# Block-sparse attention and a low-rank mixer on one core: Strassen's product for the second layer of batches 1 and 2, the mixer's second factor on row halves, casts on ScalarE

## The chip, the core and the metric

The program runs on one core of a Trainium2 chip. Its engines work side by side, each through its own instructions in order: TensorE (PE: matrix products, with its weight loads shown as PEld), VectorE (DVE), ScalarE (ACT), GpSimd (POOL), and the queue SP, which here only issues DMAs. Engines wait for each other by semaphores. Products go to PSUM, which has eight banks of 512 fp32 values in each of 128 partitions; the other operands lie in SBUF. The metric is the device time of one execution in microseconds (us).

## What is computed

Four batches, 768 tokens, 8 heads of 64. First attention with a mask that is fixed in blocks of 32 and has three sampled blocks in each block row, then a mixer of rank 32 over the tokens, then a two-layer network with a residual:

```python
scores = scale * np.matmul(q, k.transpose(0, 1, 3, 2))
...
attn = attn / (np.sum(attn, axis=-1, keepdims=True) + 1e-09)
return np.matmul(attn, v).astype(np.float32)
...
xt = x.transpose(0, 2, 1)
h = xt @ U @ V
u = x + h.transpose(0, 2, 1)
ch = np.maximum(u @ w_ch1, 0.0) @ w_ch2
return (u + ch).astype(np.float32)
```

`x` is the attention output with its heads side by side (768x512), `w_ch1` is 512x2048, `w_ch2` 2048x512. The output is fp32; the kernel multiplies in fp16 and adds in fp32.

## The kernel before

**Order.** PE, DVE, ACT and SP run in an order written out by hand: the string `PLAN`, whose words are taken one after the other. A capital letter issues PE work (or SP work), a small letter the step on DVE or ACT that belongs to an earlier product; a digit in a capital word is the PSUM bank, and words with dots carry their arguments. Each engine runs its own part of that order and waits only for data and for free buffers, so a word's place fixes its place in its engine's queue and nothing else. POOL is left to the scheduler: it casts the loaded q, k, v to fp16 (L138, L141).

**Attention.** Sixteen pairs of heads, four to a batch (`HP` = 4). For pairs 4 to 15, `Q` makes scores for both heads (`half_quad`, L890: weights of 64 rows, the two heads on the two row halves of the array, banks 0 to 2 and 3 to 5), `e` takes the exponential on ACT (L899), `p` multiplies by the mask on DVE (L905), `V` multiplies by v for one head (L401: 36 products of 65 columns). `v` divides (`divide`): a reciprocal and two products on DVE (L495), one into the fp16 tile `xh`, one into the fp32 tile `xf`. Pair n+1's transposed q and k come by DMA transposes on SP (`front`, L374), followed there by the loads of pair n+2 (L149, L160); these are issued from `divide`.

**Mixer.** `M` (`mix_all`, L584) multiplies the four `xh` of a batch by U: 24 products, four at a time on column groups of 32, giving one 128x512 sum in which each group of 32 rows holds a partial sum over some tokens. `m` copies it to fp16 (L589). `D` (`part_of_mix`, L547) multiplies by V: eight groups of three products of 128 columns and 128 rows of contraction, the four partial sums being added because V stands four times in `Vt`. `d` adds each result to `xh` (L559) and to `xf` (L560) on DVE; after the second half of a pair the transposed `xh` goes to `uT` by a DMA transpose on SP (L562). Batch 0 has other forms of this (`ut_x`, `ut_a`, `sum_only`, `add`).

**Two layers.** `U` (`w1`, L605): four products of 384 columns into a bank, then `a` (ACT, L617) or `b` (DVE, L619) takes max(x, 0) into a tile of 128x384 from a pool of 36. `W` (`w2`, L629): four products of 512 columns, four `W` to one 128-token row block of the output; `f` adds `xf` (L637) and stores 128x512 (L638) from a pool of two tiles `of`. The layers of batch b run beside the attention of batch b+1.

**Batch 3** has no attention beside it. Both its layers use Strassen's product in Winograd's form: 7 products of half size in place of 8, with sums of the operands on DVE. `q` makes the weights' sums (`weight_sum`, kept in `sw` and `tw`), `t` the inputs' sums (`input_sum`, into the mask tile), `g`, `c`, `o`, `r` the first layer (`up`, `up_copy`, `up_out`, `up_relu`), `s` the sums of the hidden layer (`token_sum`), `h` the second layer (`down`: two products of 256 columns) and `e` with dots adds into `xf` and stores (`down_out`, L792 and L794). All these products have one line, L692.

## Time and profile before

| what | value |
|---|---|
| median of 3 runs | 280.19 us (278.72 to 281.11) |
| profiled execution, its device time | 278.77 us |
| its span from first to last instruction | 277.0 us |
| PE busy | 268.9 us, 97% of the span |
| DVE busy | 227.3 us, 82% |
| ACT busy | 184.9 us, 67% |
| POOL busy | 79.2 us, 29% |
| granted TensorE clock | 1.000 |
| `M` of batch 1, 2, 3 on PE | at 95.14, 157.50, 219.90 us |
| first product of batch 3's Strassen form on PE | about 235.6 us |

The table's stretches are bounded by the `M` of each batch: from 95 to 157.5 us the layers of batch 1 run beside the attention of batch 2, from 157.5 to 219.9 those of batch 2 beside the attention of batch 3, and what follows is the rest of batch 2 and all of batch 3. A duration in a group of instructions is from the start of one instruction to its own end; where instructions of an engine follow each other closely they overlap, so the distance from start to start is shorter than the duration, and busy time counts such an overlap once.

### The profile page before, as it was taken

The numbers are of one execution on the slowest core, as the hardware profiler recorded it, in microseconds if no ns is written. First come the engines' busy times: TensorE is split into PE (matmuls) and PEld (weight loads), VectorE is DVE, ScalarE is ACT, GpSimd is POOL, SyncE is SP. The second block draws the span as 40 slices with busy tenths as digits, with TensorE's granted clock in tenths as the row PEclk, the third lists the DMA queues.
The fourth block names the chain that finished last, engine by engine and source line by source line (L and its number), as shares of the span: only waits on it lengthen the run. The fifth ranks groups of instructions, "written<-read, shape, count | busy, mean of one in ns | idle before, by whom it ended". The sixth has DMA issues, their size and how long they took to land.

```text
span 277.0 us, 6877 instructions
## 1 busy us (share of the span) xinstructions
PE 268.9 (97%) x2792; PEld 163.2 (59%) x2792; DVE 227.3 (82%) x434; ACT 184.9 (67%) x224; POOL 79.2 (29%) x164
## 2 busy tenths in 40 slices
PE   7899999999999999999999999999999999999993
PEld 3577775656464654656464654656455764566883
DVE  5699988998988898878777898798787894899972
ACT  3999998887687656678776566778876420799000
POOL 5379024915558050062725050053000000000000
PEclk9999999999999999999999999999999999999999
DMA  5799998999672474557181564552011134100024
GB/s 166 233 321 287 205 254 197 159 203 246 211 200 106 113 205 104 133 173 200 67 227 40 123 200 99 129 179 57 2 38 40 40 60 131 38 0 5 19 76 136
DMA packets 49697, 37.56 MB, mean 136 GB/s; under 512 B 30528, under 2 KB 46816, under 8 KB 49664
## 3 DMA queue, kind: packets, MB, share of 16 engines
q1 hardware_dynamic: 46688, 32.67, 42.6%
q0 software_dynamic: 2688, 4.19, 8.9%
q8 instruction: 22, 0.36, 0.6%
q10 hardware_dynamic: 288, 0.24, 0.3%
q14 instruction: 11, 0.09, 0.1%
HBM read 27.67 MB, written 6.29 MB: 123 GB/s over the span
## 4 chain that ended last, share of the span: by engine, by line
PE 92%; DVE 4%; DMA 1%; issue 1%; ACT 1%; SPq 0%; DVEq 0%; ACTq 0%
PE ps L605 23%; PE ps L629 23%; PE ps L692 13%; PE ps L401 12%; PE ps L890 10%; PE ps L846 3%; PE ps L865 2%; PE ps L547 2%; DMA qld<-in_q_dram 1%; DVE res L835 1%; PE ps L805 1%; PE ps L819 1%; DVE res L280 1%; ACT est L873 1%; PE ps L584 0%
## 5 line engine op out<-in xcount | busy, mean ns | idle before, releaser
L899 ACT ACTIVATE est<-ps 128x1536 f16<-128x1536 f32 x72 | 100.3, 1449 | 38.6 <-PE ps L890 38.6
L905 DVE TENSOR_TENSOR est<-est,mask 128x1536 f16<-128x1536 f16 x72 | 69.9, 976 | 11.7 <-ACT est L899 11.4
L605 PE MATMUL ps<-uT,w1t 128*128 128x384 f16 x384 | 72.1, 326 | 0.0
L629 PE MATMUL ps<-w2t,tT 128*128 128x512 f16 x288 | 68.3, 380 | 0.0
L605 PEld LDWEIGHTS <-w1t 128*128 128x128 f16 x384 | 35.1, 98 | 27.2 <-issue 5.8
L629 PEld LDWEIGHTS <-tT 128*128 128x128 f16 x288 | 26.7, 98 | 31.2 <-issue 3.8
L401 PEld LDWEIGHTS <-est 128*128 128x128 f16 x1152 | 40.8, 97 | 7.0 <-issue 1.9
L401 PE MATMUL ps<-vt,est 128*128 128x65 f16 x1152 | 43.4, 193 | 0.0
L617 ACT ACTIVATE tT<-ps 128x384 f16<-128x384 f32 x66 | 31.3, 496 | 16.3 <-PE ps L605 15.4
L141 POOL CAST stqld<-qld 128x192 f16<-128x192 f32 x40 | 17.9, 488 | 83.0 <-DMA qld<-in_q_dram 50.8
L890 PE MATMUL ps<-qpl,kpl 64*128 64x512 f16 (+1 forms) x288 | 31.3, 325 | 0.0
L855 ACT ACTIVATE est<-ps 128x768 f16<-128x768 f32 x30 | 22.5, 813 | 0.6 <-PE ps L846 0.6
L619 DVE TENSOR_SCALAR tT<-ps 128x384 f16<-128x384 f32 x30 | 16.6, 554 | 6.1 <-PE ps L605 5.4
L890 PEld LDWEIGHTS <-kpl 64*128 64x128 f16 x288 | 11.7, 94 | 15.9 <-issue 10.4
L141 POOL CAST stkld<-kld 128x192 f16<-128x192 f32 x40 | 20.0, 541 | 1.2 <-DMA kld<-in_k_dram 1.2
L495 DVE TENSOR_TENSOR xh<-ps,rcp 128x384 f16<-128x384 f32 x32 | 17.8, 557 | 1.1
L495 DVE TENSOR_TENSOR xf<-ps,rcp 128x384 f32<-128x384 f32 x32 | 17.5, 547 | 0.0
L141 POOL CAST vt<-vld 128x192 f16<-128x192 f32 x40 | 16.6, 458 | 0.7 <-DMA vld<-in_v_dram 0.7
L559 DVE TENSOR_TENSOR xh<-xh,ps 128x384 f16<-128x384 f16 x28 | 15.3, 548 | 1.7 <-PE ps L547 1.6
L637 DVE TENSOR_TENSOR of<-xf,ps 128x512 f32<-128x512 f32 x18 | 12.3, 682 | 4.5 <-PE ps L629 3.6
L560 DVE TENSOR_TENSOR xf<-xf,ps 128x384 f32<-128x384 f32 x28 | 15.3, 546 | 0.0
L846 PE MATMUL ps<-res 128*128 128x384 f16 x60 | 14.0, 325 | 0.8 <-DVE res L280 0.5
(111 smaller groups left out, 283.6 us busy)
## 6 DMA issues: line engine op xcount, KB each, us to landing
vld<-in_v_dram SPq DMA_DIRECT2D x16, 384.0 KB, 4.5
qld<-in_q_dram SPq DMA_DIRECT2D x15, 384.0 KB, 5.2
kld<-in_k_dram SPq DMA_DIRECT2D x15, 384.0 KB, 4.6
out_dram<-of SPq DMA_DIRECT2D x18, 256.0 KB, 2.2
w1t<-in_moe_w_ch_dram POOLq DMA_DIRECT2D x4, 512.0 KB, 8.8
w2t<-in_moe_w_ch_dram POOLq DMA_DIRECT2D x4, 512.0 KB, 7.9
out_dram<-xf SPq DMA_DIRECT2D x12, 128.0 KB, 1.7
qld<-in_q_dram SPq DMA_DIRECT2D x2, 192.0 KB
```

Source lines behind the costliest of these rows:

```text
L141: last = nc.gpsimd.tensor_copy(out=dst[:, h, ts], in_=ld[:, h, ts])
L401: nc.tensor.matmul(pav[:, sc, :], est[:, n, sc * P : (sc + 1) * P], vts[b % 2][:, 2 * hp + h, g, 0 : D + 1], start=(g == 0 and sc == 0), s ...
L495: nc.vector.tensor_tensor(out=dst, in0=pav[:, :, 0:D], in1=rcp[:, :, None].broadcast_to([P, T, D]), op=ALU.mult,)
L605: nc.tensor.matmul(pt, w1t[:, cc, jj * P : (jj + 1) * P], bts[b].uT[:, cc, c * HS : (c + 1) * HS], start=(cc == 0), stop=(cc == NCC - 1), ...
L617: nc.scalar.activation(out=dst, in_=pt, func=AF.Relu)
L629: nc.tensor.matmul(po, tts[b, c, jj][:, s * P : (s + 1) * P], w2t[:, jj, :], start=(jj == 0), stop=(jj == NJJ - 1),)
L692: nc.tensor.matmul(acc[key], lhsT, rhs, start=(first and i == 0), stop=(i == len(pairs_) - 1), skip_group_check=True,)
L846: nc.tensor.matmul(ps[:, c], kT[:, h, g * P : (g + 1) * P], qT[:, h, c * HS : (c + 1) * HS], start=True, stop=True,)
L855: lambda: nc.scalar.activation(out=dst, in_=ps, func=AF.Exp, scale=0.125),
L890: nc.tensor.matmul(units[h][:, u * S + lo : u * S + hi], kT[drows[h], g * P : (g + 1) * P], qT[drows[h], lo:hi], start=True, stop=True, sk ...
L899: nc.scalar.activation(out=both[h], in_=units[h].rearrange("p (g n) -> p g n", g=2), func=AF.Exp, scale=0.125,)
L905: lambda: nc.vector.tensor_mul(out=both[h], in0=both[h], in1=mask[:, 2 * j : 2 * j + 2, :]),
```

## The change

What it does, by parts.

1. **Second layer of batches 1 and 2.** `W` (L629) is replaced by `H` (`pair_down`). The six row blocks of 128 tokens are taken in three pairs (`tau`); each pair is a 2x2 block product, done by Strassen's seven products. `S` (`pair_sum`) makes four sums of the hidden layer for each pair (128x1024 fp16 on DVE), three into one of four slots of a new tile `sums`, the third in place. One `H` is four products of 256 columns; 14 `H` make a pair. `D` (`pair_out`) adds each of seven results (128x256) into `xf`, and `Z` stores a row block of `xf`; `of` and `f` remain for batch 0 alone.
2. **The hidden layer's tiles.** The pool of 36 tiles is gone: `relu` writes into one tile `hid` with a place for each of 2x16 results, used by batches 0 to 2 one after the other, and by batch 3 for the sums of its hidden layer.
3. **Weights' sums.** `tw` (sums of `w_ch2`, now needed from batch 1 on) lies where `sw` was, and `sw` (sums of `w_ch1`, for batch 3) in the load tiles. The words `q.3` to `q.5` and `q.7` move ahead to batch 1, `q.0` to `q.2` back to batch 3.
4. **Mixer's second factor.** `mix_all` keeps its 24 products but puts them in 256 columns: each row half of the sum belongs to two pairs of heads. `F` (`mix_parts`) multiplies 64 rows at a time, three products on the upper half and three on the lower, alternating, into two banks; four `F` make a batch. `m` copies 128x256.
5. **Casts on ScalarE.** For batches 2 and 3 `v` writes `xf` alone and `y` copies it to `xh` on ACT. For batches 1 to 3 the mixer's sum is added into `xf` alone on DVE (`x`) and `d` copies it into `xh` on ACT.
6. **Placement.** From batch 1 on each relu, transpose (`T`), load of a pair (`L`), store (`Y`, `Z`) and finish (`f`) has its own word with its own engine, bank and place. The pool of `of` has one tile.

Its core, from the diff:

```diff
-    tpool = ctx.enter_context(tc.tile_pool(name="tpool", bufs=36))
-    opool = ctx.enter_context(tc.tile_pool(name="opool", bufs=2))
+    opool = ctx.enter_context(tc.tile_pool(name="opool", bufs=1))
+    hid = consts.tile([P, 2, 16, HS], FP16, name="hid")
+    NSUM = 4
+    sums = consts.tile([P, NSUM, NJJ // 2, P], FP16, name="sums")
...
+            if self.b > 1:
+                then("y", lambda: nc.scalar.copy(out=xh, in_=xf))
+            for dst in (xh, xf)[self.b > 1 :]:
...
+        def add_part(self, c):
+            xf = self.bt.xf[:, 3 * c : 3 * c + 3, self.ch]
+            nc.vector.tensor_add(out=xf, in0=xf, in1=self.pu[c])
+
+        def cast_part(self, c):
+            ts = slice(3 * c, 3 * c + 3)
+            nc.scalar.copy(out=self.xh[:, ts, :], in_=self.bt.xf[:, ts, self.ch])
...
-        then("m", lambda: nc.vector.tensor_copy(out=bt.a16, in_=pa))
+        then("m", lambda: nc.vector.tensor_copy(out=bt.a16[:, 0 : 2 * P], in_=pa))
+
+    def mix_parts(b, k, *ns):
+        u, c = divmod(k, 2)
+        for h, n in enumerate(ns):
+            pairs[b * HP + 2 * h + u].pu[c] = bank(n, [P, 3, P], FP32)
+        for j in range(3):
+            for h in range(2):
+                rows = slice(h * RH, (h + 1) * RH)
+                nc.tensor.matmul(
+                    pairs[b * HP + 2 * h + u].pu[c][:, j, :],
+                    Vt[rows, 3 * c + j, :],
+                    bts[b].a16[rows, u * P : (u + 1) * P],
+                    start=True, stop=True, skip_group_check=True,
+                )
...
+            dst = tts[b, c, jj] = hid[:, c, jj]
...
+    def quads(tau):
+        lo, hi = (divmod(t, T // 2) for t in (2 * tau, 2 * tau + 1))
+        return [
+            hid[:, c, u : u + NH, s * P : (s + 1) * P]
+            for (c, s), u in ((lo, 0), (lo, NH), (hi, 0), (hi, NH))
+        ]
+
+    def pair_sum(b, tau, k, n=None):
+        a11, a12, a21, a22 = quads(tau)
+        if k != 3:
+            slot_of[b, tau, k] = sums[:, n]
+        s1, s2, s4 = (slot_of.get((b, tau, m)) for m in (1, 2, 4))
+        if k == 1:
+            nc.vector.tensor_add(out=s1, in0=a21, in1=a22)
+        else:
+            minus(nc.vector, *{2: (s2, s1, a11), 3: (a21, a11, a21), 4: (s4, a12, s2)}[k])
+
+    def pair_down(b, tau, p, part, n=None):
+        a11, a12, a21, a22 = quads(tau)
+        a = {1: a11, 2: a12, 4: a22, 7: a21}.get(p)
+        if a is None:
+            a = slot_of[b, tau, {5: 1, 6: 2, 3: 4}[p]]
+        terms = []
+        for j in range(part * NH // PARTS, (part + 1) * NH // PARTS):
+            w = tw[:, {4: 2, 5: 0, 6: 1}[p], j] if p in (4, 5, 6) else w2_part(p, j)
+            terms.append((a[:, j], w))
+        product((ACC[p], b, tau), terms, p in (1, 2, 5) and part == 0, n)
+
+    def pair_out(b, tau, k):
+        a, u, col = {
+            0: ("X", 0, 0), 1: ("Y", 0, 0), 2: ("X", 0, 1), 3: ("X", 1, 1),
+            4: ("B", 1, 1), 5: ("X", 1, 0), 6: ("B", 0, 1),
+        }[k]
+        row, ch = 2 * tau + u, slice(col * DM, (col + 1) * DM)
+        x = bts[b].xf[:, row, ch]
+        nc.vector.tensor_add(out=x, in0=x, in1=acc[a, b, tau])
```

The words of the new `PLAN` around the `M` of batch 2 (the `F` up to the first `U` of that batch), and from the `M` of batch 3 to its first products:

```
S.1.1.1.2 v y y y H.1.1.1.0.7 H.1.1.1.1 H.1.2.1.0.5 H.1.2.1.1 S.1.2.1.3 v y
S.1.1.2.0 D.1.1.0 y H.1.0.2.0.0 S.1.2.2.1 M6 H.1.0.2.1 D.1.2.0 H.1.2.6.0 L.10 L.11 m H.1.2.6.1
S.1.2.3 D.1.0.1 F.2.0.6.2 F.2.1.1.3 F.2.2.0.4 D.1.2.2 H.1.2.7.0 x.10.0 d.10.0 x.10.1 x.9.0 d.9.0
H.1.2.7.1 D.1.2.3 H.1.2.2.0.2 x.8.0 F.2.3.3.0 d.8.0 x.11.0 x.9.1 d.11.0 d.10.1 x.8.1 d.8.1 T.10 T.8
x.11.1 d.11.1 T.11 d.9.1 T.9 H.1.2.2.1 H.1.2.4.0 H.1.2.4.1 Z.1.0.0 H.1.1.2.0.6 H.1.1.6.0 H.1.1.6.1
H.1.1.2.1 D.1.2.5 D.1.2.1 Q S.1.1.3 D.1.1.2 H.1.1.7.0 D.1.1.1 H.1.1.7.1 H.1.2.5.0.6 H.1.2.5.1 e e
D.1.1.3 H.1.1.4.0 S.1.2.4.3 H.1.1.4.1 D.1.2.4 Q D.1.1.5 H.1.2.3.0 e e H.1.1.5.0.7 S.1.1.4.1
H.1.2.3.1 D.1.2.6 H.1.1.5.1 U.2.0.8.2 U.2.0.13.6
...
S.2.2.3 D.2.1.2 M3 D.2.2.0 D.2.2.1 H.2.1.2.0.2 m H.2.1.2.1 S.2.1.3 F.3.0.6.3 F.3.1.4.5 x.12.0
...
H.2.1.3.1 g.2.1.2 D.2.2.6 g.0.1.4 q.6.1 t.1 g.1.1.1 D.2.1.6 g.3.1.6 c.2.1.7 t.2 c.0.1.2 g.0.2.5
```

In a word, `H.b.tau.p.part.bank` names the product, `S.b.tau.k.slot` the sum, `F.b.k.bank.bank` the two banks, `x.i.c`, `d.i.c` and `T.i` the pair of heads.

More of the change, by code (lines that the diff above doesn't have):

```diff
@@ L593 @@
     held = {}
+    relus, finishes = {}, {}
     XP = 2
@@ L619, in relu, with store @@
                 nc.vector.tensor_scalar_max(out=dst, in0=pt, scalar1=0.0)
-        then("relu", relu)
+        if (b, c, jj) > (0, 1, 10):
+            relus[b, c, jj] = relu
+        else:
+            then("relu", relu)
+    finished = {}
+    def store(b, sc, x=None):
+        x = finished[b, sc] if x is None else x
+        nc.sync.dma_start(
+            out=out[b].rearrange("(p t) d -> p t d", t=T)[:, sc, :], in_=x
+        )
     def w2(b, sc, part, n=None):
@@ L637, in finish @@
                 nc.vector.tensor_add(out=of, in0=bts[b].xf[:, sc, :], in1=po)
[L638 to L645 removed]
+                if sc < 3:
+                    store(b, sc, of)
+                finished[b, sc] = of
+            if sc < 3:
+                then("f", finish)
+            else:
+                finishes[b, sc] = finish
+    sw = {}
+    tw = res.rearrange("p a b s -> p (a b s)").rearrange(
+        "p (k j d) -> p k j d", k=3, j=NJJ // 2
     )
[L647 removed]
     tu = mask[:, 0:4, :].rearrange("p k (c n) -> p k c n", c=2)
@@ L800 @@
         "h": down, "e": down_out, "q": weight_sum,
+        "F": mix_parts, "U": lambda b, c, jj, n: w1(b, c, jj, n), "W": w2,
+        "x": lambda i, c: pairs[i].add_part(c), "d": lambda i, c: pairs[i].cast_part(c),
+        "a": lambda b, c, jj, e: relus.pop((b, c, jj))("ba"[e]),
+        "f": lambda b, sc: finishes.pop((b, sc))(),
+        "T": lambda i: pairs[i].turn(), "L": lambda i: loads(i + 1), "Y": store,
+        "Z": lambda b, tau, u: store(b, 2 * tau + u, bts[b].xf[:, 2 * tau + u]),
+        "S": pair_sum, "H": pair_down, "D": pair_out,
     }
```

163 lines of the change are left out of this document (90 added, 73 removed).

## The prediction

> **What bounds the kernel now.** I read the page's busy shares and its chain that ended last first, then the busy time in stretches of 20 us, then the chain in order of time, then single instructions on PE and DVE.
>
> From the page, busy time by engine and the chain's shares:
>
> ```profile
> PE 268.9 (97%) x2792; PEld 163.2 (59%) x2792; DVE 227.3 (82%) x434; ACT 184.9 (67%) x224; POOL 79.2 (29%) x164
> ...
> PE 92%; DVE 4%; DMA 1%; issue 1%; ACT 1%; SPq 0%; DVEq 0%; ACTq 0%
> ```
>
> Busy time by stretch (length, PE, PEld, DVE, ACT, POOL, granted clock, DMA share, GB/s):
>
> ```profile
> 140.00:160.00 20.00, 20.00 (x266) 11.90 (x264) 15.32 (x26) 12.75 (x13) 5.75 (x12) 1.00 0.48 139
> 160.00:180.00 20.00, 20.00 (x192) 11.17 (x190) 16.76 (x31) 12.67 (x16) 3.58 (x12) 1.00 0.53 134
> 220.00:240.00 20.00, 19.58 (x141) 10.59 (x133) 15.69 (x31) 5.29 (x12) 0.00 (x0) 1.00 0.31 79
> 240.00:260.00 20.00, 20.00 (x142) 13.75 (x141) 18.48 (x53) 15.81 (x36) 0.00 (x0) 1.00 0.01 2
> ```
>
> From 60 us on PE has no idle time but 0.42 us near 237 and the tail after 272.8. So what PE sheds there is saved, unless another engine then makes it wait; DVE is nearest to that, at 92% from 240 to 260. A busy PE could still be a slow one, so I read what a product costs where products follow each other. The chain in order of time (start, length, what):
>
> ```profile
> 108.88 3.56 PE ps L629 x16
> ...
> 132.50 0.76 PE ps L890 x8
> ...
> 135.95 0.65 PE ps L605 x4
> 136.60 0.76 PE ps L890 x8
> 137.35 0.76 PE ps L605 x4
> ...
> 140.49 1.09 PE ps L401 x36
> ...
> 224.43 0.84 PE ps L547 x15
> ...
> 226.78 8.65 PE ps L629 x40
> 235.58 0.47 issue
> 236.05 1.03 DVE mask L653 x2
> 237.13 35.64 PE ps L692 x272
> ```
>
> Single instructions, products of 256 columns on PE and sums on DVE (start, duration, what):
>
> ```profile
> 268.88 1.04 PE L692 MATMUL ps<-w2t,tT 128*128 128x256 f16 x8
> 269.75 1.04 PE L692 MATMUL ps<-tw,est 128*128 128x256 f16 x8
> ...
> 222.43 0.55 DVE L560 TENSOR_TENSOR xf<-xf,ps 128x384 f32<-128x384 f32 x1
> 222.90 0.55 DVE L559 TENSOR_TENSOR xh<-xh,ps 128x384 f16<-128x384 f16 x1
> ```
>
> Unit prices: 512 columns 8.65/40 = 0.216 us; 384 columns 0.65/4 = 0.163; 256 columns (269.75 - 268.88)/8 = 0.109; 128 columns 0.84/15 = 0.056. On DVE the distance from start to start is 0.47 where the duration is 0.55: I take 0.085 off each DVE duration. ACT's copies come 0.36 to 0.39 apart (duration 0.49).
>
> **The change, part by part.**
>
> *Second layer.* Per batch it removes 6 row blocks x 16 = 96 products of 512 columns, 96 x 0.216 = 20.8 us, and adds 3 pairs x 7 x 8 = 168 of 256 columns, 168 x 0.109 = 18.3. Two batches: 4.9 us less on PE, all in stretches where PE sets the time. The 72 more weight loads a batch are hidden: L401 loads 128x128 weights for each of its products and passes 36 in 1.09 us, 0.030 each, well under 0.109. "TensorE: Matmul & The Clock Gate" of the Trainium skill (Back-to-back issue gap) has in a real stream of loads and products 131 ns at 512 columns and 81 at 128; by that, with an estimate of 98 at 256 columns from its line between the two, a batch would go from 12.6 to 16.5 us and the two lose 7.8. This trace disagrees, with 216 and 109 ns in long streams.
>
> *Mixer.* Per batch eight groups of three products of 128 columns (24 x 0.056 = 1.34) become four `F` of six half-height products. L890 shows that two row halves run together: four of 512 and four of 256 would be 1.30 one by one and take 0.76, ideally 0.65. So an `F` is 3 x 0.056 = 0.17, bounded below by weight loads at 6 x 0.030 = 0.18; three batches go from 4.0 to 2.1. But each change of the tiling costs: L890 takes 0.11 over its ideal, and the four L605 behind it 0.76 in place of 0.65. The twelve `F` stand in six runs between full-height products (in each batch's plan two runs), 6 x 0.22 = 1.3. Net gain 0.6; ends: 1.9 if the changes are free, a loss of 1.3 if the halves do not overlap. I take 0.6, as L890 shows both effects. "TensorEngine Tiling (Array Packing)" of the skill (Key Properties) says that changing the tiling mode drains the engine; the 0.11 before and behind agree.
>
> *DVE.* Away: 16 divisions into `xh` (0.47), 24 additions into `xh` (0.46), 12 `f` (0.60), and 0.3 to 0.4 on each of three `m`: 26.9 us. Added: 42 `D` at 0.33 (L792, 0.415 less 0.085) = 13.9; 24 `S` of 1024 fp16, 0.60 by L653 on `w2t` with POOL idle, 0.74 by its 0.83 us beside POOL: 14.4 to 17.8, I take 0.65, 15.6; two more `r` of each size and one relu, 1.3. Sum: 4 us more, 227 to 231, with PE's span down to 271: 85%. Counted word by word between the `M`s, DVE has 47.8 us for batch 1 (before 48.2), 52.6 for batch 2 (49.3) and 42.1 behind (42.2), beside PE's 60.2, 60.4 and 46.5. It fits on average, most tightly behind: with tiling changes PE takes about 48 us there, so DVE's idle time must shrink from 10.7 us (52.9 - 42.2) to 6. I set 0.5 us of PE's waiting for that, between 0 and the 2.9 us by which DVE's part from the first `g` on grows (four `D` 1.3, one `q` 0.7, `r` 0.9).
>
> *ACT.* 40 casts at 0.39 (L725's 0.494 less 0.11; L743's 0.541 from SBUF as upper end) = 16 us more, 2 us less of `r`: 199 of 271. Hidden while scores run. They lengthen the way to the next batch, below.
>
> *Waits that are added.* The way from `M` to the next `U` is `m`, `F`, eight `x`, the last `d`, four transposes on SP. At batch 2, from the words: `m` 0.4, `F` 0.2, eight `x` 3.7, four `D` and an `S` between them 1.9, `d` 0.4, one transpose queued before the last 1.2 (L562), landing 2.8: 10.6 us. PE has 12.3 us between (22 `H` at 0.44, four `F`, two `Q` at 0.87). Batch 1 has 18 us. Batch 3 has 9.5, but its first products need only the first two pairs, which land some 2 us earlier. `L.10` and `L.11` stand before these transposes on SP, but they need only the last scores of pairs 10 and 11 and the casts, done before `M`; before, `front` and the loads (154.33 to 160.5) stood there too. So no wait, with a margin of a microsecond or two. Before `M`, a new one: after `V4` of batch 2 DVE has p 0.89, S 0.60, v 0.69, S 0.60, v 0.69, then ACT's y 0.39, 3.9 us, against V2 and five `H` on PE, 3.3: 0.6 us of wait; the like at batch 3. Together 1.0 rounded down, and with the 0.5 above 1.5.
>
> The single `of` makes `f.0.4` wait for store `Y.0.3`: landing 2.2 behind an issue of 0.36 and a transpose of 1.2, 3.8 us; PE has three `W` and a `Q`, 3.5 us, before `f.0.4` could run anyway. `f.0.5` may wait 1.2 behind `T.6` and `T.7`; queued behind it on DVE are `v` and PE's bank 6, needed 1.8 us later. Nothing lost; 1 us if that cover is gone. The weights' sums move within stretches where DVE is free for 13 us in 62.
>
> *Sum.* 278.77 - 4.9 - 0.6 + 1.5 = 274.8 us for an execution like the profiled one, which lies 1.4 under the median of the runs shown (280.19). A median would lie between 274.8 and 276.2; I say 275.4.
>
> **Rivals.**
>
> 1. *PE sheds its work, and the pair sums give it back.* Each of six pairs starts with `S1`, whose result product 5 needs, and ends with `S4`. If PE meets one sum (0.6) of each on the way, 3.6 us go: 274.8 becomes 278.4, within 1% of 280.19. Against it: PE has four products that need no sum (1, 2, 4, and 7 after `S3`), and the plan puts them between.
> 2. *DVE becomes the bound: slower.* In the trace DVE is idle for 14.1, 13.1 and 10.7 us of the three stretches (62.3 - 48.2, 62.4 - 49.3, 52.9 - 42.2), because masks wait for exponentials and sums for products. If that idle time cannot shrink, the stretches last 61.9, 65.7 and 52.8 us: +2.8 in sum, 281.6 for the profiled kind, 283 for a median. It decides from the point where batch 2's idle time stays above 62.4 - 52.6 = 9.8 and the last one does not shrink. For it: DVE's 92% at 240 to 260. Against it: at 240 to 260 PE runs without a gap at that load.
> 3. *Half the columns do not halve a product's time*, because the next weights come late: a load's row is 98 ns long, and the skill's rule above speaks for such a cost. If a product of 256 columns took 0.109 plus even a fifth of a load, 0.129, a batch would take 21.7 in place of 20.8: +1.8 against the 4.9 forecast, 281.0. The L692 rows with new weights at each product speak against it.
> 4. *Only the mixer pays or only the tiling's changes cost*: the second layer gains 4.9 and the mixer loses 1.3: 276.7, inside the forecast's range.
>
> **How the numbers follow.** Forecast with variant 4: 0.73. Rival 1: 0.12. Rival 2: 0.10. Rival 3: 0.05. What a measurement here can tell from no change is about 1%, 2.8 us: faster is below 277.4, slower above 283.0. Faster: the forecast, 0.73. Rival 1, half of rival 2 and most of rival 3 lie within 1%: 0.12 + 0.05 + 0.02 = 0.19. Slower: the other half of rival 2 and what is left of 3, 0.08. The forecast's own range is 271.5 (mixer at its upper end, 1.9, and no waits: 278.77 - 6.8 = 272.0, a little under for runs faster than the profiled one) to 277.5 (variant 4 and a microsecond more of waits). To leave out no more than 2 in 10 I go up to 280.0, which takes in rival 1.
>
> **What would show it.** PE's rows: 336 products of 256 columns 0.109 apart and 96 of 512 left; the twelve `F` at 0.17 to 0.2 each with 0.1 on either side; PE idle under 1.5 us between 70 us and its last product. `S` rows at 0.68 to 0.83. By the words between them PE has 0.5 us less up to the `M` of batch 2, another 0.4 less up to that of batch 3 and 5.4 behind (`M` of batch 3 near 219 in place of 219.9, the last product near 269 in place of 272.8). Wrong would be: PE waiting on `sums` or `hid` (rival 1), DVE at over 95% in a stretch with PE idle (rival 2), a pitch over 0.12 (rival 3), or PE waiting on `uT` after an `M`, which would say that the way over ACT and SP is longer than 10.6 us.

## The result, and the profile after

The changed kernel takes 276.07 us (median of 19 runs, 274.3 to 278.61). The kernel before, run as often beside it, takes 280.3 us (278.37 to 283.28). The ratio is 0.9856, with a 95% interval of 0.9827 to 0.9886: faster by 4.2 us. The profiled execution took 274.89 us with a span of 273.0, against 278.77 and 277.0 before.

The page after, busy time by engine and the chain's shares:

```profile
PE 264.3 (97%) x2936; PEld 174.5 (64%) x2936; DVE 229.3 (84%) x453; ACT 199.2 (73%) x259; POOL 80.7 (30%) x164
...
PE 83%; DVE 10%; DMA 3%; issue 1%; ACT 1%; SPq 0%; DVEq 0%; ACTq 0%
```

PE is busy for 4.6 us less, DVE for 2.0 and ACT for 14.3 us more. The chain goes through DVE and DMA more often, 10% and 3% against 4% and 1%. The four stretches that the prediction showed, in the view by stretch of the kernel after (length, PE, PEld, DVE, ACT, POOL, granted clock, DMA share, GB/s):

```profile
140.00:160.00 20.00, 19.83 (x302) 14.85 (x298) 17.43 (x34) 13.15 (x17) 9.44 (x24) 1.00 0.43 133
160.00:180.00 20.00, 20.00 (x215) 14.21 (x211) 15.76 (x31) 16.04 (x22) 0.32 (x2) 1.00 0.55 140
...
220.00:240.00 20.00, 19.56 (x186) 14.00 (x184) 18.39 (x42) 10.36 (x24) 0.00 (x0) 1.00 0.42 119
240.00:260.00 20.00, 20.00 (x155) 14.89 (x153) 19.27 (x59) 10.70 (x24) 0.00 (x0) 1.00 0.03 8
```

From 220 to 240 DVE's busy time grew from 15.69 to 18.39 of 20, and PE stays as busy as before (19.56 against 19.58). From 240 to 260 DVE is at 96% and PE still has no gap. The chain of the kernel after in order of time (start, length, what), where it leaves PE:

```profile
96.50 0.86 PE ps L702 x4
97.37 0.44 PE ps L645 x12
97.81 0.97 PE ps L702 x4
...
107.86 3.56 PE ps L702 x16
...
153.66 0.69 DVE sums L863
154.50 0.56 DVE xf L531
155.06 0.77 DVE sums L863
155.97 0.56 DVE xf L531
156.53 0.63 DVE sums L729
157.49 0.71 DVE sums L729
158.58 1.03 PE ps L768 x8
...
227.31 0.94 ACT xh L614 x2
228.38 4.48 DMA uT<-xh
232.98 0.57 DVE mask L729
233.60 34.10 PE ps L768 x260
```

`L702` is `W` (16 of 512 columns in 3.56 us, no faster and no slower than before), `L645` is `F`, `L768` every Strassen product. Two passages are new. Near the `M` of batch 2 (157.35) the chain runs through DVE's pair sums and batch 2's divisions, and at the end of the mixer of batch 3 through ACT's cast `d`, 4.48 us of transposes up to the last landing, and the first sum of the transposed activations (`mask`). The groups that carry the change, in the view by line and shape (line, engine, operation, tiles and shapes, count, then busy time, mean ns of one, idle time before):

```profile
L768 PE MATMUL ps<-w2t,hid 128*128 128x256 f16 x168 | 22.0, 273 | 0.0
...
L863 DVE TENSOR_TENSOR sums<-hid 128x1024 f16<-128x1024 f16 x6 | 4.4, 740 | 0.7 <-ACT hid L679 0.6
...
L729 DVE TENSOR_TENSOR sums<-hid,sums 128x1024 f16<-128x1024 f16 x6 | 4.1, 685 | 0.5 <-PE ps L768 0.5
L645 PE MATMUL ps<-a,Vt 64*128 64x128 f16 x72 | 3.1, 218 | 0.0
```

A duration of a product here is from its start to its own modelled end and says little of its price. Two neighbouring rows of products of 256 columns with new weights each, in the changed kernel (start, time, what):

```profile
224.65 1.92 PE L768 MATMUL ps<-res,sums 128*128 128x256 f16 x16
226.41 1.04 PE L768 MATMUL ps<-w2t,hid 128*128 128x256 f16 x8
```

From start to start the sixteen take 1.76 us, 0.110 each, while their mean duration is 0.273. So I measured the price from the starts: for each product the distance to the next start, less the pitch that its size has in long runs (0.216 us for 512 columns, 0.1625 for 384, 0.109 for 256, 0.056 for 128, 0.0303 for 65; half for a product on 64 rows, a quarter for one of 32 columns). What is left is put down to changes of the tile form (the rows and columns of the array that a product uses) where the next product has another form, and to waits otherwise; a wait that ends at a change of form is thus counted with the change. Summed from the `M` of batch 1 to the last product, in us:

| kernel | whole | product time | at changes of form (number) | other waits | `M` of batch 1, 2, 3 at | last product at |
|---|---|---|---|---|---|---|
| before | 177.34 | 170.5 | 7.33 (50) | -0.52 | 95.14, 157.43, 219.83 | 272.48 |
| after | 173.28 | 163.7 | 8.87 (63) | 0.74 | 95.23, 157.35, 220.86 | 268.50 |

(The pitches are rounded, so the column of waits can be negative; only its differences mean something. The changed kernel profiled a second time gave a whole of 173.14, and a variant below that differs from it at the start alone gave 172.79. So a difference of less than half a microsecond in the waits can be chance; single times spread over 4 us.) The whole shrank by 4.06 us: 6.9 less product time, 1.55 more at thirteen more changes of form, 1.26 more of waits.

### The profile page after: what moved, and what is told of

The parts are those of the page before. It is cut to its first block, busy times and chain, and to the rows that moved or that the text cites. A ratio compares the mean times of both kernels' runs of the same rounds, so it can differ in the third digit from the quotient of the medians.

```text
span 273.0 us, 7182 instructions
## 1 busy us (share of the span) xinstructions
PE 264.3 (97%) x2936; PEld 174.5 (64%) x2936; DVE 229.3 (84%) x453; ACT 199.2 (73%) x259; POOL 80.7 (30%) x164
## 4 chain that ended last, share of the span: by engine, by line
PE 83%; DVE 10%; DMA 3%; issue 1%; ACT 1%; SPq 0%; DVEq 0%; ACTq 0%
PE ps L667 23%; PE ps L768 22%; PE ps L403 11%; PE ps L1016 10%; PE ps L702 8%; PE ps L972 3%; PE ps L991 2%; DMA uT<-xh 2%; DMA qld<-in_q_dram 1%; DVE xf L610 1%; DVE res L961 1%; DVE est L1031 1%; DVE xf L531 1%; PE ps L931 1%; PE ps L645 1%
## 5 line engine op out<-in xcount | busy, mean ns | idle before, releaser
L667 PE MATMUL ps<-uT,w1t 128*128 128x384 f16 x384 | 70.7, 326 | 0.4 <-DVE xf L531 0.3
L679 ACT ACTIVATE hid<-ps 128x384 f16<-128x384 f32 x65 | 30.1, 497 | 7.3 <-PE ps L667 6.6
L768 PEld LDWEIGHTS <-hid 128*128 128x128 f16 x264 | 25.1, 98 | 4.7 <-DVE xf L887 0.6
L681 DVE TENSOR_SCALAR hid<-ps 128x384 f16<-128x384 f32 x31 | 17.2, 554 | 8.3 <-PE ps L667 7.9
L702 PE MATMUL ps<-w2t,hid 128*128 128x512 f16 x96 | 23.4, 380 | 0.0
L768 PE MATMUL ps<-w2t,hid 128*128 128x256 f16 x168 | 22.0, 273 | 0.0
L143 POOL CAST vt<-vld 128x192 f16<-128x192 f32 x40 | 21.1, 566 | 1.1 <-DMA vld<-in_v_dram 1.1
L887 DVE TENSOR_TENSOR xf<-xf,ps 128x256 f32<-128x256 f32 x42 | 16.8, 414 | 3.3 <-PE ps L768 3.2
L614 ACT CAST xh<-xf 128x384 f16<-128x384 f32 x24 | 11.3, 511 | 8.6 <-DVE xf L610 8.1
L768 PEld LDWEIGHTS <-sums 128*128 128x128 f16 x144 | 13.6, 98 | 3.8 <-issue 0.9
L702 PEld LDWEIGHTS <-hid 128*128 128x128 f16 x96 | 8.7, 98 | 10.6 <-issue 1.9
```

The costliest lines, as they stand in the source:

```text
L143: last = nc.gpsimd.tensor_copy(out=dst[:, h, ts], in_=ld[:, h, ts])
L667: nc.tensor.matmul(pt, w1t[:, cc, jj * P : (jj + 1) * P], bts[b].uT[:, cc, c * HS : (c + 1) * HS], start=(cc == 0), stop=(cc == NCC - 1), ...
L679: nc.scalar.activation(out=dst, in_=pt, func=AF.Relu)
L681: nc.vector.tensor_scalar_max(out=dst, in0=pt, scalar1=0.0)
L702: nc.tensor.matmul(po, tts[b, c, jj][:, s * P : (s + 1) * P], w2t[:, jj, :], start=(jj == 0), stop=(jj == NJJ - 1),)
L768: nc.tensor.matmul(acc[key], lhsT, rhs, start=(first and i == 0), stop=(i == len(pairs_) - 1), skip_group_check=True,)
```

## The experiments

My theory after the result: the gain is the 4.9 us of Strassen's second layer and 2.0 us of product time in the mixer, cut by the changes of form and by waits on DVE's sums, as forecast. The rivals: that the mixer's changes cost nothing, that the sums cost far more or nothing, that the casts could as well have stayed on DVE. In the expectations, "M1 to last" stands for the column "whole" above.

### The mixer's product at full height

```diff
-        pa = bank(n, [P, RH * 4], FP32)
+        pa = bank(n, [P, HD], FP32)
+        tiles = [[(c, hp) for hp in range(HP)] for c in range(4)]
+        for c in range(4):
+            tiles[c] += [(4 + c // 2, 2 * (c % 2) + u) for u in range(2)]
...
-                    Vt[rows, 3 * c + j, :],
-                    bts[b].a16[rows, u * P : (u + 1) * P],
+                    Vt[:, 3 * c + j, :],
+                    bts[b].a16[:, hp * P : (hp + 1) * P],
```

> The changed kernel with the mixer's second factor at full height again (24 products of 128 rows a batch instead of 12 pairs of half-height products), everything else as in the change. Theory (the half heights save 1.8 us of product time and pay about 1.5 us in changes of the tiling): the profiled execution is about 0.3 us slower than the changed kernel's 274.9, so 275.2, median 276.4; in the trace the sum of product times from 60 us on rises by 1.8 us and twelve or so changes of tiling (0.12 us each) disappear. Rival A (the halves save their whole 1.8 us): 276.7 profiled, median 277.9. Rival B (the changes cost more than the halves save): below 274.6 profiled.

Measured: 277.63 us against 280.68 for the kernel before, ratio 0.990 (0.9849 to 0.9951). The sum by starts is 174.21 us, 0.93 more than with half heights: product time +2.0, changes of form -1.39 (51 instead of 63), other waits +0.31. So the half-height form is worth 0.9 us, or 0.6 without the waits, which lie within the spread of these sums. That is between the theory's 0.3 and rival A's 1.8, at or a little above the prediction's 0.6, and at most half of the 2.0 that it would be if changes cost nothing. The median, 1.6 us above the changed kernel's 276.07, can't tell them apart, since single times spread more than that. One `F` pair and its neighbours on PE in this kernel (start, time, what):

```profile
100.07 0.83 PE L648 MATMUL ps<-a,Vt 128*128 128x128 f16 x12
100.74 1.03 PE L705 MATMUL ps<-w2t,hid 128*128 128x512 f16 x4
```

and in the changed kernel:

```profile
97.30 0.51 PE L645 MATMUL ps<-a,Vt 64*128 64x128 f16 x12
97.74 1.04 PE L702 MATMUL ps<-w2t,hid 128*128 128x512 f16 x4
```

From start to start twelve products take 0.67 us at full height (12 x 0.056) and 0.44 at half height. Twelve overlapping halves would be 0.34, so 0.10 us is lost at the change behind them; about as much is lost at the change ahead, where the four products of 512 columns take 0.96 us up to the first half (96.34 to 97.30) in place of 0.86. In all, the twelve changes that go away here were worth 1.39 us, 0.12 each; the thirteen of the whole change cost 1.55, also 0.12 each. The Trainium skill's "TensorEngine Tiling (Array Packing)" (Key Properties) says that a change of the tiling mode drains the engine; the 0.12 us is what that comes to here.

### No pair sums

`pair_sum` issues nothing. Each product that would read one of `sums` reads `a11`, and product 7 reads `a21` as it is. The 24 sums on DVE are left out.

```diff
     def pair_sum(b, tau, k, n=None):
         a11, a12, a21, a22 = quads(tau)
         if k != 3:
-            slot_of[b, tau, k] = sums[:, n]
...
+            slot_of[b, tau, k] = a11
```

> The changed kernel without the 24 sums of the hidden layer in batches 1 and 2; the products that used them read the hidden layer itself, so the output of those batches is not the reference's. PE's work is unchanged, DVE has 24 instructions (17 us) less. Theory (the sums are hidden but for single waits): 0.3 to 0.8 us faster than the changed kernel, 274.1 to 274.6 profiled, median near 275.5. Rival 1 (PE meets a sum in each pair): 3 us or more faster, median below 273. Rival 2 (DVE bounds the stretches): more than 5 us faster.

Measured: 274.8 us, ratio 0.9797 (0.9739 to 0.9855); by starts 171.93, which is 1.35 less than the changed kernel. Of this 1.2 is in other waits and 0.15 at changes of form, product time is equal; the profile lists no idle time of PE between the `M` of batch 1 and the last product. So the 24 sums, 16.8 us of busy time on DVE by their rows, cost PE 1.35 us, which is more than my theory's 0.3 to 0.8 and well short of rival 1's 3. The sums account for nearly all of the waits that the change added (1.26). The profiled execution doesn't show the gain (275.7 us): ahead of the part that is summed here, at 75.74 us, PE sat idle for 1.87 us in front of a `W` of batch 0, where the changed kernel has no gap. No run shows whether that belongs to the edit.

### The eighth product of each pair put back

Product 2 of each pair is done twice, so that a pair has as much product time as the plain form of the kernel before (64 of 256 columns for 32 of 512).

```diff
+        if p == 2:
+            terms = terms + terms
         product((ACC[p], b, tau), terms, p in (1, 2, 5) and part == 0, n)
```

> The changed kernel with an eighth product in each of the six pairs: product 2 is issued twice into its bank (the output of batches 1 and 2 counts it twice). 48 products of 256 columns more. Theory (PE bounds these stretches, a product of 256 columns costs 0.109 us): 5.2 us slower than the changed kernel, 280.1 profiled, median 281.3; so Strassen's missing eighth product is worth its whole time. Rival (another engine already sets part of the time): 0 to 3 us slower, median below 279.

Measured: 280.03 us over 12 runs, against 280.68, ratio 0.9988 (0.9947 to 1.0029). By starts 177.28: 4.0 more than the changed kernel for 5.2 us more product time; waits fell by 1.1. The theory had the whole 5.2, the rival 3 at most. With the eighth product in it the whole change, its sums, casts, mixer and placement, gives nothing that can be measured; the gain is the product that Strassen leaves out, worth 4.0 us net here, since the longer product time covers 1.1 us of waits.

### All casts back on DVE

`y` issues nothing and the division writes both `xh` and `xf` on DVE; the mixer's sum is added on DVE into both; `d` is empty.

```diff
-                then("y", lambda: nc.scalar.copy(out=xh, in_=xf))
-            for dst in (xh, xf)[self.b > 1 :]:
+                then("y", lambda: None)
+            for dst in (xh, xf):
...
         def add_part(self, c):
             xf = self.bt.xf[:, 3 * c : 3 * c + 3, self.ch]
+            xh = self.xh[:, 3 * c : 3 * c + 3, :]
+            nc.vector.tensor_add(out=xh, in0=xh, in1=self.pu[c])
...
-            nc.scalar.copy(out=self.xh[:, ts, :], in_=self.bt.xf[:, ts, self.ch])
+            pass
```

> The changed kernel with the 40 casts taken off ScalarE: DVE writes xh itself from PSUM, as before the change (divisions of batches 2 and 3, additions of batches 1 to 3), right beside the write of xf. DVE gets 40 more instructions at 0.47 us, 18.6 us. Theory (DVE has little room left, 84% of the span, and the way from one batch to the next has only a microsecond of margin at batch 2 and less than none at batch 3): PE waits 2 to 5 us, median 278 to 281, with the waits on uT after the mixer of batches 2 and 3. Rival (DVE has room enough, the casts need not have moved): within 0.7 us of the changed kernel, median 275.4 to 276.8.

Measured: 290.38 us, ratio 1.036 (1.0305 to 1.0414), slower than the kernel before. By starts 186.47: 13.2 more than the changed kernel, of which 8.1 in other waits and 5.1 at changes of form. My theory was right that PE would wait, and wrong in two things: the size, 13.2 us where it had 2 to 5, and the cause, since none of PE's waits behind the `M` of batch 1 is on `uT`; all are on DVE, most of them for a bank of PSUM that `x` or `D` had to read. The rival, that DVE has room enough, falls. The view by stretch of this kernel, bounded by its `M`s (columns as above):

```profile
96.66:163.11 66.45, 63.42 (x691) 38.18 (x690) 55.60 (x98) 44.30 (x48) 24.05 (x55) 1.00 0.50 140
163.11:232.29 69.18, 64.02 (x750) 43.80 (x750) 61.67 (x114) 44.49 (x50) 8.38 (x18) 1.00 0.24 64
232.29:283.13 50.84, 47.82 (x408) 36.19 (x408) 47.73 (x128) 16.76 (x38) 0.00 (x0) 1.00 0.22 66
```

DVE is at 84%, 89% and 94% of the stretches: not full, and yet PE is idle for 3.0, 5.2 and 3.0 us. The mean load alone does not explain PE's waits. The next two runs look for the place.

### Only the mixer's additions, and only the divisions, on DVE

The second and third part of the last diff alone (additions), and its first part alone (divisions).

> The changed kernel with only the mixer's 24 casts taken back: the sums of batches 1 to 3 are added into xh on DVE, beside xf, and nothing is cast on ScalarE there; the casts after the divisions stay on ScalarE. Read from the mixer product of batch 1 to the last product (173.3 us in the changed kernel, 186.5 with all 40 casts on DVE). Theory (the loss of 13.2 us lies on the way from the mixer to the next batch's first layer: eight more instructions of 0.47 us behind each mixer product, 3.7 us, three times): 183 to 185 us, with PE's waits in the 12 us behind each mixer product. Rival (DVE is too full everywhere): about 24/40 of the loss, 181 us, spread over the stretches.

> The changed kernel with only the 16 casts after the divisions of batches 2 and 3 taken back to DVE; the mixer's casts stay on ScalarE. Read from the mixer product of batch 1 to the last product (173.3 us in the changed kernel). Theory (these 16 are off the way from batch to batch but for the last two of a batch): 174 to 175.5 us. Rival (DVE is too full everywhere): about 16/40 of the 13.2 us, 178.6 us.

Measured: with the additions on DVE 285.47 us in a single run, by starts 182.92, or 9.6 more; with the divisions on DVE 279.48 us in a single run, by starts 177.64, or 4.4 more. PE behind the `M` of batch 2 (161.33) with the additions on DVE (start, time, what; in brackets the idle time before and its releaser):

```profile
165.91 0.21 PE L646 MATMUL ps<-a,Vt 64*128 64x128 f16 x1 [0.33 <-DVE xf L612]
166.84 0.32 PE L646 MATMUL ps<-a,Vt 64*128 64x128 f16 x5 [0.72 <-DVE xf L612]
...
171.82 1.05 PE L1017 MATMUL ps<-qpl,kpl 64*128 64x512 f16 x8 [1.49 <-DVE xf L612]
173.41 1.82 PE L769 MATMUL ps<-w2t,hid 128*128 128x256 f16 x8 [0.54 <-DVE xf L888]
```

The stretches of this run from that `M` on, and the first twelve microseconds behind the same `M` in the changed kernel (columns as above):

```profile
161.33:173.40 12.07, 8.95 (x109) 6.67 (x109) 12.07 (x28) 0.51 (x1) 3.09 (x8) 1.00 0.21 43
173.40:175.00 1.60, 1.59 (x8) 1.12 (x8) 0.29 (x1) 1.60 (x2) 0.00 (x0) 0.53 0.79 153
175.00:176.90 1.90, 1.90 (x11) 1.32 (x9) 0.42 (x1) 0.68 (x1) 0.00 (x0) 0.50 0.53 165
...
157.35:169.40 12.05, 11.88 (x141) 8.99 (x140) 10.80 (x26) 6.59 (x10) 2.97 (x8) 1.00 0.28 50
```

Not all of the 9.6 us is DVE's. From 173.4 to 176.9 us the granted clock was 0.53 and 0.50, and sixteen products of 256 columns lay 0.21 us apart in place of 0.109; that alone is some 1.7 us. With all casts on DVE PE waits as long at the same place and the clock stays at 1.00, so the low clock is an accident of this execution as far as the runs show. Without it the additions cost 7.9 us, and the two parts add up to 12.3, against the 13.2 of both at once.

For the additions the theory had the place right. Every idle time of PE that the profile lists from the `M` of batch 1 on lies within 12.1 us behind an `M`, and in the 12.07 us shown DVE is busy without a gap while PE works for 8.95; with the casts on ACT DVE is busy for 10.80 of 12.05 us and PE for 11.88. A queue of some 12 us in which DVE is full sets the time there, whatever its share of the stretch. In size 7.9 is below the 9.7 to 11.7 that the theory stands for (183 to 185) and near the rival's 7.7 (181). For the divisions the rival came nearer, in size (4.4, against its 5.3 and the theory's 0.7 to 2.2) and in kind: only two of the nine idle times of PE that the profile lists, of 1.04 and 0.77 us, lie behind an `M` (within three microseconds), and the other seven, of 0.2 to 0.4 us each, are spread over the stretches. So the larger part of the loss is the queue behind `M`; the rest lies partly there and partly where DVE is short of room elsewhere.

### The halves one after the other in program order

```diff
-        for j in range(3):
-            for h in range(2):
+        for h in range(2):
+            for j in range(3):
```

> The changed kernel with the half-height products of the mixer's second factor in another order: three on the upper row half, then three on the lower, instead of alternating. Read from the mixer product of batch 1 to the last product (173.3 us in the changed kernel), as the start of the kernel varies. Theory (the halves overlap only where neighbours lie on different halves): four of the six products of an F no longer overlap, each F takes 0.28 us instead of 0.17, twelve F 1.3 us, so 174.6 us. Rival (the array overlaps them in any order, or did not overlap them before): 173.3 within 0.2.

Measured: 277.25 us in a single run, by starts 173.21: unchanged. The theory (174.6) falls and its rival holds. Twelve such products on PE in this kernel:

```profile
99.80 0.52 PE L645 MATMUL ps<-a,Vt 64*128 64x128 f16 x12
100.25 1.04 PE L702 MATMUL ps<-w2t,hid 128*128 128x512 f16 x4
```

They take 0.45 us from start to start, as in alternation. Starts of the first six, in us:

```
in turn      99.798  99.808  99.865  99.875  99.921  99.931
alternating  97.300  97.303  97.366  97.370  97.422  97.426
```

Both run in pairs, with 56 to 67 ns from pair to pair. The trace doesn't print the row half of a product, but its records carry the marks of the semaphores: of the first six, the fifth and the sixth to start raise one in both kernels, while the last products into the two banks are the third and the sixth of the program when the halves come in turn. So I read each pair as one product of each half: with three products on the upper rows ahead of three on the lower ones in program order, the second half still starts 10 ns behind the first. The two halves keep their own order, and not one order in common.

### Another order of `x` and `D`, and one store for two row blocks

Two of the waits that the trace of the changed kernel shows were attacked: 0.75 us on the way to batch 3's first sums, by placing `x.15` and `d.15` ahead of two `D`; and a gap on DVE near 180 us, by storing two row blocks of `xf` in one DMA (three stores a batch instead of six).

```diff
-    d.12.1 d.14.0 d.14.1 x.13.1 H.2.1.5.0.3 d.13.0 d.13.1 D.2.2.2 H.2.2.5.0.4 D.2.1.3 H.2.1.5.1 x.15.1
-    H.2.2.7.0 x.15.0 d.15.0 T.12 H.2.2.7.1 D.2.2.3 H.2.2.5.1 T.14 H.2.1.4.0 S.2.2.4.0 d.15.1 H.2.2.4.0
+    d.12.1 d.14.0 d.14.1 x.13.1 H.2.1.5.0.3 d.13.0 d.13.1 x.15.1 x.15.0 d.15.0 d.15.1 D.2.2.2 H.2.2.5.0.4 D.2.1.3 H.2.1.5.1
+    H.2.2.7.0 T.12 H.2.2.7.1 D.2.2.3 H.2.2.5.1 T.14 H.2.1.4.0 S.2.2.4.0 H.2.2.4.0
...
-        "Z": lambda b, tau, u: store(b, 2 * tau + u, bts[b].xf[:, 2 * tau + u]),
+        "Z": lambda b, tau, u: store_pair(b, tau),
```

> The changed kernel with two edits that go at its two visible waits. In the last stretch DVE adds the two parts of pair 15 (x.15.1, x.15.0) before the sums D.2.2.2 and D.2.1.3, so that the last transpose into uT starts some 0.7 us earlier; and the twelve stores of batches 1 and 2 become six of double size, so that the first division of batch 3, which reuses the xf tile of batch 1, waits for three semaphores instead of six. Theory: the wait of 0.75 us at batch 3's first sums of uT shrinks by 0.5 or more, the one of 0.47 us behind the first V of batch 3 by 0.2 or more; from the mixer product of batch 1 to the last product 172.4 to 172.8 us instead of 173.3, median some 0.7 us under the changed kernel's 276.1. Rival: PE then waits as long for D.2.2.2 and D.2.1.3, and the semaphores are not what the division waits for: 173.3 within 0.3.

Measured: 273.45 us, ratio 0.980 (0.9749 to 0.9851); by starts 172.33, 0.95 less than the changed kernel, all of it in other waits. DVE near 180 us in the changed kernel:

```profile
179.81 0.20 DVE L525 RECIPROCAL rcp<-ps 128x6 f32<-128x6 f32 x1 [0.81 <-PE ps L403]
180.50 0.56 DVE L531 TENSOR_TENSOR xf<-ps,rcp 128x384 f32<-128x384 f32 x1 [0.49 <-DVE rcp L525]
```

and with three stores:

```profile
179.53 0.20 DVE L525 RECIPROCAL rcp<-ps 128x6 f32<-128x6 f32 x1 [0.82 <-PE ps L403]
179.77 0.56 DVE L531 TENSOR_TENSOR xf<-ps,rcp 128x384 f32<-128x384 f32 x1
```

and in the kernel without pair sums, which has six stores again:

```profile
181.56 0.20 DVE L525 RECIPROCAL rcp<-ps 128x6 f32<-128x6 f32 x1 [0.81 <-PE ps L403]
181.89 0.56 DVE L531 TENSOR_TENSOR xf<-ps,rcp 128x384 f32<-128x384 f32 x1
```

The profile names the reciprocal as the releaser of the 0.49 us, but that had ended at 180.01. The `xf` of batch 3 reuses the tile of batch 1; the first write to it stands behind three instructions that wait for six semaphores, one for each store. The last of the stores had landed two microseconds earlier, so it is not their data that is waited for. With three stores the gap is gone, and with it 0.47 us of waiting on PE. But the six waits alone are not the cause: without pair sums the same three instructions with the same six semaphores stand there, and the write starts 0.13 us behind the reciprocal (181.76 to 181.89). With the additions on DVE it is 0.13 us too, while six other profiles of kernels with six stores have 0.48 or 0.49. What the remaining 0.36 us is stays open. Stores and order were changed together here; the traces tell their places apart. The other half of the run only moved a wait: the sums of the transposed activations now run without one, but PE waits 0.35 us (0.51 by the starts) near 226 us for one of the `D` that was moved back.

### The changed kernel again, and a longer warm-up

The times of the changed kernel come in groups, near 274.6, 276.1 and 277.2 us. One run is the changed kernel as it is; one does ten products at the start of the program where the kernel does eight; one has the last section's edits and the ten.

```diff
-        keep_warm(8)
+        keep_warm(10)
```

> The changed kernel itself again, for comparison on the same chip with the next two. Both theories: its times fall into groups near 274.6, 276.1 and 277.2 us, as in its 19 runs so far.

> The changed kernel with ten instead of eight products of 512 columns that warm PE up before the first q arrives, so that PE has no idle time of 0.8 us before 5.2 us. Theory (the groups of times come from the moment at which PE goes to full rate: the first products after 5.2 us take 0.14 us a piece in slow starts and 0.09 in fast ones, and a gap in PE's work decides it): the group near 277.2 disappears, most runs lie near 274.6, median below 275.3. Rival (the moment does not depend on PE's work before 5.2 us): the three groups stay, median 275.5 to 276.5.

> The ten warm-up products, the order of the last stretch's sums and the stores of double size together. Theory: 0.9 to 1.0 us under the kernel with ten warm-up products alone, median near 274, and faster than the kernel before by 2.2%. Rival (the two edits only had fast starts in their first test): no difference from the kernel with ten warm-up products; but the time from the mixer product of batch 1 to the last product, which the start does not touch, must then be 173.3 again instead of 172.3.

| kernel | median (range), us | ratio to before (95%) | whole, us | first score pair of batch 1 at |
|---|---|---|---|---|
| after, second time | 275.59 (274.45 to 277.41) | 0.9867 (0.9816 to 0.9919) | 173.14 | 46.09 |
| ten products | 275.06 (274.55 to 275.95) | 0.9848 (0.9799 to 0.9896) | 172.79 | 43.72 |
| ten, order and stores | 273.61 (273.36 to 277.75) | 0.9794 (0.9748 to 0.9841) | 172.38 | 44.05 |

The second profile of the changed kernel took 277.41 us where the first took 274.89, and its first score pair of batch 1 comes 2.6 us later (46.09 against 43.49), while the whole from `M` on is the same to 0.14. The difference arises at the start. The first products of the changed kernel in its first profile:

```profile
0.79 3.57 PE L267 MATMUL ps<-const-bfloat16-1.0 128*128 128x512 bf16 x8 [0.79 <-PEq L1162]
5.20 0.52 PE L227 MATMUL ps<-small,stqld 128*64 128x128 f16 x6 [0.84 <-DVE stqld L213]
```

and in its second:

```profile
0.79 3.57 PE L267 MATMUL ps<-const-bfloat16-1.0 128*128 128x512 bf16 x8 [0.79 <-PEq L1162]
5.33 0.85 PE L227 MATMUL ps<-small,stqld 128*64 128x128 f16 x6 [0.97 <-DVE stqld L213]
```

The same six products take 0.52 us in one and 0.85 in the other, behind the same warm-up and an idle time of 0.84 and 0.97 us; the profile's granted clock is 1.00 at both starts. The low rate lasts: up to about 12.5 us the products of the second profile stay nearly twice as far apart (0.32 us against 0.16 for 384 columns), by then it is 2.6 us behind, and this distance no longer changes. The two profiles explain the outer two groups of times; the middle one has no profile. With ten products:

```profile
0.79 4.14 PE L267 MATMUL ps<-const-bfloat16-1.0 128*128 128x512 bf16 x10 [0.79 <-PEq L1162]
5.07 0.52 PE L227 MATMUL ps<-small,stqld 128*64 128x128 f16 x6
```

The idle time is gone, the six run at 0.52, and the six runs lie within 1.4 us. "TensorE: Matmul & The Clock Gate" of the Trainium skill (Part 1) says that the clock's window runs freely, so that the moment at which it opens differs between runs of the same program; the two rates after an equal warm-up agree with that, though no run shows the window itself. Six runs are few, and the longer warm-up doesn't settle whether the idle time decides the rate: in the profile of the third kernel of the table the first six products took 0.84 us again, and one of its runs took 277.75 us. The edits of order and stores, with and without the longer warm-up, beat the changed kernel in the median by 2.0 to 2.6 us and by 0.8 to 0.95 us in the sums by starts; the rest of the difference in medians I put down to which starts were drawn. Against the kernel with ten products alone the gain in the sums is 0.41 us, where 0.9 to 1.0 was expected: that kernel's sum is itself 0.35 to 0.5 under the changed kernel's, with nothing changed behind the start. The gap on DVE is gone in both kernels with three stores; the size of both edits together is known to half a microsecond only.

## Why the prediction was right

The forecast for an execution like the profiled one was 274.8 us, and it took 274.89. That it came so close is in part luck, as the terms show. The sum was 4.9 + 0.6 - 1.5; its terms came out as follows.

**Second layer, 4.9.** Right. Between the `M` of batch 1 and the last product the product time fell by 6.9 us, which is 4.9 for `H` against `W` and 2.0 for the mixer, where 4.9 and 1.9 were forecast. The 256-column products lie 0.11 us apart, with new weights for each, so rival 3 falls. (By its own terms that rival comes to 281.5 us and not 281.0.) The Trainium skill's 131 and 81 ns ("TensorE: Matmul & The Clock Gate", Back-to-back issue gap) don't hold here either, as the prediction had judged. The eighth product shows that the gain is this one.

**Mixer, 0.6.** Right. Product time 2.0 less, 1.9 forecast; changes of form 1.55 in place of 1.3, or 1.39 by the run at full height, which leaves 0.6. That run also had 0.3 us more of other waits, by which the net is 0.9. Variant 4, a loss of 1.3, falls.

**Waits, 1.5.** The sum was right (1.26, and 1.35 for the sums alone by the run without them), the places were partly wrong. Forecast were 0.6 us ahead of each of two `M`, and 0.5 in the last stretch. The `M` of batch 2 and that of batch 3 follow their neighbours with no gap. By the starts the stretches between the `M`s have 0.20, 0.98 and 0.07 us more of waits than before: nearly all of it lies between the `M` of batch 2 and that of batch 3. There 0.34 us shows just behind the first (a bank that a `D` had to empty, ahead of the products at 158.58) and 0.47 near 181. In the last stretch 0.53 us ahead of the product at 233.60 and 0.22 just before stand against 0.58 at the like place before, so little was added. In the trace after, it reads:

```profile
232.98 0.56 DVE L729 TENSOR_TENSOR mask<-uT,mask 128x768 f16<-128x768 f16 x1 [1.05 <-DMA uT<-xh]
```

That is not the wait on DVE's load which the prediction gave as the reason for its 0.5, but the one it had ruled out and named as a sign of being wrong, on the way from `M` over `x`, `d` and the transpose. It took this way as 10.6 us long, 6.6 up to the end of the last `d` and 4.0 for the transposes (1.2 of queue and 2.8 to land), against 9.5 us of other work on PE at batch 3, with the first two pairs some 2 us sooner. At batch 3 the last cast ends about 7.4 us behind the `M` (220.86 to 228.25), and the transposes take 4.48 more: 12.0 in all, 1.4 over the forecast, which is about the margin that it had allowed. PE lost 0.75 us of it. At batch 2, no wait on `uT` came, as forecast.

A wait that the prediction did not see at all is the 0.47 us near 181 us, for the tile of `xf` that is used again behind six stores; of the gap on DVE behind it, 0.49 us, at most 0.13 is shown to be the six waits. That the waits forecast at the wrong places and those left out came to the same sum is luck.

**Rival 1** (sums give it back, 3.6) had the right mechanism at a third of its price: 1.35. **Rival 2** (DVE becomes the bound) did not happen. DVE's idle time could shrink where it had to, between the `M` of batch 2 and that of batch 3 from 11.2 us to 8.9 and in the last stretch from 8.6 (52.65 less 44.08 busy) to 4.3 (47.64 less 43.34). How near it was is shown by the run with all casts on DVE: 17 us more busy time on DVE (246.3 against 229.3) made the part from the `M` of batch 1 to the last product 13.2 us longer. What the prediction lacked is where the edge is: it weighed DVE by stretches of 50 to 60 us, and for the additions, the larger part of that loss, the edge lies in the 12 us behind each `M`.

**Smaller points.** ACT's casts last 0.51 us from `xf` in SBUF, between the two rows that bounded them (0.494 and 0.541). The sums last 0.685 to 0.74 us, within the 0.68 to 0.83 forecast. `of` had DVE wait 3.0 us for the store, more than the 1.2 forecast, and PE lost nothing, as forecast. The `M` of batch 3 was forecast near 219 and came at 220.86, later than before (219.83). The products were counted well: by the starts their time fell by 0.6, 0.7 and 5.6 us in the three stretches, forecast 0.5, 0.4 and 5.4. But the count left out the changes of form and the waits, and between the `M` of batch 2 and that of batch 3 these grew by 0.8 and 1.0 us. The last product came at 268.5, forecast near 269. The median came out 0.7 us above the 275.4 that I gave, and 1.2 above the profiled execution; I put that down to the start, by how many runs begin at the lower rate; the runs that are not profiled can't show it.

## What to carry to other kernels

When PE is busy without a gap, price a change there by the distance from start to start in long streams; the sum of such pitches was right to a tenth of a microsecond, where durations and shares would not have been. Work that goes to another engine for it must fit the stretch of some ten microseconds where that engine already has a queue, and not the mean alone: at 84% the pair sums cost PE 1.35 us, while eight more additions on DVE behind each `M`, where it was then full for 12 us, cost about 8 us in all. Look at the granted clock of each stretch before a loss is put down to a wait: 1.7 us of the additions' loss was a slow clock. To learn what a part is worth, put its saving back alone (the eighth product): that told the source of the gain in one run.

## What the hardware did that I had not expected

- Products on the two 64-row halves overlap in both orders that were run: with three and three in turn, the second product of each pair (by the semaphores' marks the other half's) starts 10 ns behind the first, and twelve take 0.45 us, as when they alternate (0.44).
- Six equal products behind an equal warm-up take 0.52 us in one execution and 0.85 in another, with the clock shown as full in both; the low rate lasts to about 12.5 us, and by this the whole program comes out 2.6 us later.
- In one execution the granted clock fell to 0.50 in the middle of the program, from 173.5 to 176.9 us, behind 12 us in which PE had been busy for 8.95; another kernel with as many waits at the same place kept 1.00.
- The first write to a tile that six stores have read stood 0.48 or 0.49 us behind its last operand in six profiles and 0.13 in two others, with the same six waits and all stores landed; with three stores 0.03.
